# A linear-attention and MLP kernel on one core: the first kv in narrow columns, a quotient taken ahead, and loads moved

## Chip, core and metric

The kernel runs on one core of a Trainium2 chip. The metric is the device time of one execution in microseconds, the median of the runs shown. All arithmetic is float32.

## What is computed

The reference is an attention with a polynomial sketch as its feature map, followed by a layer norm and a two-layer MLP with a residual. Batch 4, 4 heads, sequence 1088, head size 32, r = 8, so 64 features; model size 128, hidden size 512.

```python
def phi(x):
    a = np.einsum('rd,bhsd->bhsr', S1, x)
    b = np.einsum('rd,bhsd->bhsr', S2, x)
    return np.einsum('bhsi,bhsj->bhsij', a, b).reshape(*x.shape[:-1], r * r)
q_p, k_p = (phi(q), phi(k))
kv = np.einsum('bhsf,bhsd->bhfd', k_p, v)
z = np.sum(k_p, axis=2)
num = np.einsum('bhsf,bhfd->bhsd', q_p, kv)
den = np.einsum('bhsf,bhf->bhs', q_p, z)[..., None] + 1e-06
x = (num / den)          # heads side by side: (B, S, 128)
...
xn = (x - mu) / np.sqrt(var + 1e-06) * g_ln
out = x + np.maximum(xn @ w_ch1, 0.0) @ w_ch2
```

## The kernel before

The program is written out by hand: every engine executes its instructions in the order in which the code emits them, and a wait of one instruction holds all that stand behind it on the same engine. The engines are TensorE (PE), VectorE (DVE), ScalarE (ACT), GpSimd (POOL) and SyncE (SP), which issues nearly all DMAs. DMAs of a queue share eight semaphores in turn, so that a DMA can also wait for the one eight places ahead of it.

The work is cut in two ways. Keys and values are taken by batch: for each of the four batches `key_rows` transposes the keys on DVE (tile kT), `key_features` multiplies them by the sketch on PE, `key_products` forms the 64 products per head and token (tile kp, mostly on POOL), `key_tokens` copies the values beside a column of ones (tile v), and `key_values` accumulates kv and z for the batch in one PSUM bank and copies the result to SBUF (kvz). The copy is made thrice: once as it stands, and twice with the two halves of the partitions exchanged[...].

Queries are taken in nine chunks of up to 512 tokens (two for each batch, and a last one with the 64 left over tokens of all four). For each chunk, query features are formed (from chunk 4 on by `token_products`, then through DRAM by `write_products` and `read_products`, tiles qo, qrows and qx). `numerators` multiplies them by kvz in 64x64 tiles on PE, and divides on DVE (tiles den, rden, x). `turn_x` or, through DRAM, `send_x` and `blocks_x` (tiles rows and xb) transpose x to xT; `hidden` is the first MLP layer (L620), `second` the second (L633), `result` adds the residual and sends the output.

At the start everything waits for loads. `load_rows`, `load_part`, `load_v` and `load_w1` issue them all at once on SyncE: batch 0's keys, queries and values, g, w1 in two halves, then w2, the rest of batch 0's queries, and batches 1 to 3 in order. w1 must be centred and scaled by g (`first_weight`). The weights come as 64-bit floats: the class `Rounded` splits each into a rounded float and a rest (methods `sizes`, `bound`, `terms`), and `one` adds the two. `busy` issues a multiplication without use, which fills TensorE's queue.

After that a loop runs over the slots c = 2 to 8. In slot c the kernel does the MLP of chunk c, the quotients of chunk c + 2, and the query products of chunk c + 4; keys enter beside it. The keys and values of batch 3 are transposed and copied at the end of slot 2 (`keys_in(3)`), their features and products are formed in slot 3 (`keys(3, ...)`), and their kv in slot 4 (`key_values(3, ...)`). In SyncE's order slot 2 is: outputs of chunk 1, qx of chunk 5, qrows of chunk 6, rows of chunk 4, xb of chunk 4, qx of chunk 6; then the outputs of chunk 2.

Of the kernel before, what the change touches and what calls it, by code (L numbers as in the profile page):

```python
# [10 lines left out]
U32 = mybir.dt.uint32  # L11
# [18 lines left out]
def kernel(  # L30
# [34 lines left out]
    nc = tc.nc  # L65
    P = 128
    B, H, S, D = q.shape
    R = S1.shape[0]
    DM = H * D
# [20 lines left out]
    def bank(i):  # L90
        return banks[:, 512 * i : 512 * (i + 1)]
# [14 lines left out]
    def load_rows(t, src, b, c0=0, c1=G * D):  # L106
        nc.sync.dma_start(  # L107
            out=t[b][:, c0:c1],
            in_=bass.AP(
                src.tensor, src.offset + b * H * S * D + c0, [[G * D, P], [1, c1 - c0]]  # L110
            ),
        )
# [41 lines left out]
    def load_w1(cols):  # L154
# [1 line left out]

    load_w1(slice(0, 256))
    load_w1(slice(256, DH))
    nc.sync.dma_start(
        out=w2_raw.rearrange("p (jc f) -> p jc f", f=DM),  # L160
        in_=moe_w_ch2.rearrange("(jc p) f -> p jc f", p=P),
    )
    load_rows(qn, q, 0, 512)
    load_rows(kn, k, 1)
    for b in range(1, B):
        if b > 1:
            load_rows(kn, k, b)
        load_v(b, nc.sync, lambda p0: 8 * p0, 8, 0)
        load_v_rest(b, nc.sync)
        load_rows(qn, q, b)  # L170


    class Rounded:
# [73 lines left out]
    def busy(n, at=0):  # L247
        nc.tensor.matmul(  # L248
            bank(at)[:, 0:n], ones, _ap(ones, 0, P, 0, [[0, n]]), start=True, stop=True
        )  # L250
# [55 lines left out]
    def key_tokens(b, part, eng, i0=0, i1=4):  # L306

        t0, n, m = (4 * part + i0, i1 - i0, P) if part < 2 else (8, 1, 64)
        o = _ap(v1s[b % 2], 0, m, t0 * W, [[W, n], [D1, H], [1, D]])
        i = _ap(vn[b], 0, m, D * t0 if part < 2 else 8 * DM,  # L310
                [[D, n], [8 * D if part < 2 else D, H], [1, D]])
        if eng is nc.scalar:
            eng.copy(o, i)
        else:
            eng.tensor_copy(out=o, in_=i)
# [31 lines left out]
    def key_values(b, at, t0=0, t1=NT):  # L347

        kvp, v1, kp, kvz = bank(at), v1s[b % 2], kps[b], kvzs[b]


        step = 64 if b == 0 else 32
        for t in range(t0, t1):
            m = P if t < 8 else 64
            for f in range(0, H * F, step):
                h, o = f // F, f % P
                nc.tensor.matmul(  # L357
                    kvp[o : o + step, D1 * (h // 2) : D1 * (h // 2 + 1)],
                    kp[0:m, H * F * t + f : H * F * t + f + step],
                    v1[0:m, W * t + D1 * h : W * t + D1 * (h + 1)],  # L360
                    start=(t == 0 and h < 2), stop=(t == NT - 1), skip_group_check=True,
                )
        if t1 < NT:
            return
        nc.scalar.copy(kvz[:, 0 : 2 * D1], kvp[:, 0 : 2 * D1])
        for i in range(2):
            nc.scalar.copy(  # L367
                kvz[F * i : F * i + F, 2 * D1 : W],
                kvp[F * (1 - i) : F * (2 - i), 0 : 2 * D1],
            )  # L370

    qTs, qos, qrs, qxs, qps = {}, {}, {}, {}, {}
    xs, rs, mvs, xTs, hTs, xbs = {}, {}, {}, {}, {}, {}
# [108 lines left out]
    def numerators(c):  # L482


        if c > LAST:
            return
        x = xs[c] = work.tile([P, 512], F32, tag="x", name="x", bufs=4)
        qp, n = qps.pop(c), ntiles(c) // 2
        step = 64 if c < LAST else 32
        for i in range(n):  # L490
            for h in range(H):
                for half in range(2):
                    rows = slice(F * half, F * half + F)
                    for u in range(0, P, step):
                        kvz = kvzs[CHUNKS[c][0] if c < LAST else u // 32]
                        t, o = 256 * h + P * i + u, W * i + D1 * h
                        z = D1 * (h // 2) + (0 if h % 2 == half else 2 * D1)
                        nc.tensor.matmul(  # L498
                            bank(half)[u : u + step, o : o + D1], qp[rows, t : t + step],
                            kvz[rows, z : z + D1], start=True, stop=True,  # L500
                        )
        den = small.tile([P, 4 * H], F32, tag="den", name="den")
        rden = small.tile([P, 4 * H], F32, tag="rden", name="rden")
        m = n * H
        nc.vector.tensor_scalar(
            out=_ap(den, 0, P, 0, [[m, 2], [1, m]]),
            in0=_ap(banks, 0, P, D, [[512, 2], [D1, m]]),
            scalar1=1e-6, scalar2=None, op0=ALU.add,
        )
        nc.vector.reciprocal(rden[:, 0 : 2 * m], den[:, 0 : 2 * m])  # L510
        for half in range(2):
            by_i, by_h = x_steps(c)
            nc.vector.tensor_tensor(  # L513
                out=_ap(x, 0, P, by_i * n * half, [[by_i, n], [by_h, H], [1, D]]),
                in0=_ap(banks, 0, P, 512 * half, [[W, n], [D1, H], [1, D]]),
                in1=_ap(rden, 0, P, m * half, [[H, n], [1, H], [0, D]]),
                op=ALU.mult,
            )
# [191 lines left out]
    key_tokens(0, 0, nc.gpsimd, 2, 4)  # L710
    key_tokens(0, 1, nc.vector)
    key_tokens(0, 2, nc.gpsimd)

    def rest():
        busy(128, 7)
        key_features(0, 2, 6)
        key_products(0, 2, nc.vector)

    query_features(0, rest)
    halves = [slice(0, 256), slice(256, 512)]  # L720
    w1_parts.sizes(halves[0], True)
    key_values(0, 7)
    busy(128, 4)

    g_terms = all_terms(g_raw, "g", 1)
    g_f = g_terms[0]
# [4 lines left out]
    nc.gpsimd.tensor_scalar(  # L731
        out=center, in0=ident, scalar1=-1.0 / DM, scalar2=g_f, op0=ALU.add, op1=ALU.mult
    )
    w1_parts.bound(halves[0], nc.vector)
    w1_term = one(w1_parts.terms(halves[0]), nc.vector)
    w1_parts.sizes(halves[1], True)
    w1_parts.bound(halves[1], nc.gpsimd)
    numerators(0)
    first_weight(halves[0], w1_term)
    turn_x(0)  # L740
    w2_parts = parts(w2_raw, "w2")
# [93 lines left out]
    for c in range(2, LAST + 1):  # L835

        b = (c + 3) // 2
        odd, some = c % 2 == 1, b < B
        if c == LAST - 1:
            blocks_x(LAST)  # L840
        if c < LAST:
            mlp_in(c, {
                1: lambda: key_values(b, 7, 0, 5), 3: lambda: key_values(b, 7, 5)
            } if some and not odd else {})
            root(c)
        if c == LAST - 1:
            root(LAST)
        numerators(c + 2)
        write_products(c + 4)
        send_x(c + 2)  # L850
        read_products(c + 4)
        if some and odd:
            keys(b, (2, 3, 7))
        statistics(c + 2)
        if c < LAST - 1:
            blocks_x(c + 1)
        if c == LAST - 1:
            second(c, 0, 3)
            result(c, 0, 3)
            mlp_in(LAST, {})  # L860
            second(c, 3, 4)
            result(c, 3, 4)
        else:
            second(c)
            query_rows(c + 5)
            result(c)
        token_products(c + 5)
        query_products(c + 3)
        if b + 1 < B and not odd:
            keys_in(b + 1)  # L870
# [30 lines left out]
```

## Time and profile before

| | us |
|---|---|
| median of 3 runs | 112.9 (112.32 to 114.01) |
| the profiled execution | 111.67 |
| its span, first to last instruction | 109.9 |
| TensorE busy | 102.4 (93%) |
| VectorE, GpSimd, ScalarE busy | 66.6, 49.1, 38.8 |

A profile is of one execution. "Busy" counts the time in which an engine has an instruction under way; fp32 products are done in two passes, so that TensorE has two records and two weight loads for each multiplication of the program. In a timeline a line gives the start from the beginning of the span, the duration, the engine, the line of the code, the operation, output and inputs, and how many instructions were merged; in brackets stands the idle time of the engine before it and what ended it. An engine with a q behind its name means its queue, such as SPq for DMAs issued. The chain is followed back from the last instruction, at each step to what released it; "issue" in it is time in which the engine waited for nothing that the profile shows. Line numbers are those of the code printed above.

### The profile page before, as it was taken

Reading aid. Unit: us, or ns where it says so; the run is one execution under the profiler, and the core shown is the slowest. Engines: PE = TensorE matmul, PEld = TensorE weight load, DVE = VectorE, ACT = ScalarE, POOL = GpSimd, SP = SyncE. Lnnn points to the kernel's source line nnn. Section 1 sums busy time; section 2 is a strip of 40 time slices with the busy share of each in tenths; the row PEclk is TensorE's granted clock in tenths of the full one; section 3 lists DMA queues with packets and bytes.
Section 4 is the critical chain, followed back from the end, with each engine's and each line's share of the span. In section 5 each row is a group of like instructions: output and inputs, shape, how many; then the busy total and the mean of one; then the engine's idle time right before and its main releaser. Section 6 shows DMA issues by size and latency. Waiting matters only on the chain.

```text
span 109.9 us, 4466 instructions
## 1 busy us (share of the span) xinstructions
PE 102.4 (93%) x1881; PEld 72.6 (66%) x1881; DVE 66.6 (61%) x196; ACT 38.8 (35%) x94; POOL 49.1 (45%) x139
## 2 busy tenths in 40 slices
PE   6899959999999799999999999999999999999960
PEld 3367825589745398855794698549829829839950
DVE  1776998994997476492389766707556546320330
ACT  5126317724557250225303530261062062062500
POOL 4065124006995099999443989702402404204000
PEclk9999999999999999999999999999999999999999
DMA  0999899999995206472987298518426434140032
GB/s 15 290 199 251 268 277 218 313 191 227 272 217 150 61 9 145 102 236 66 207 286 250 66 292 254 131 56 331 138 63 226 134 83 140 47 134 9 0 80 63
DMA packets 15155, 17.85 MB, mean 162 GB/s; under 512 B 3872, under 2 KB 10528, under 8 KB 15136
## 3 DMA queue, kind: packets, MB, share of 16 engines
q1 hardware_dynamic: 15040, 17.51, 58.8%
q8 instruction: 14, 0.23, 0.9%
q10 hardware_dynamic: 96, 0.07, 0.2%
q14 instruction: 5, 0.04, 0.2%
HBM read 11.54 MB, written 6.03 MB: 160 GB/s over the span
## 4 chain that ended last, share of the span: by engine, by line
PE 81%; DVE 5%; DMA 4%; SPq 3%; issue 2%; ACT 1%
PE banks L633 30%; PE banks L620 30%; PE banks L498 7%; PE banks L357 5%; DMA vn<-in_v_dram 4%; PE banks L322 3%; PE banks L403 3%; PE banks L429 2%; PE banks L580 1%; SPq L128 1%; DVE qp L412 1%; SPq L116 1%; DVE w_rest L687 1%; SPq L107 0%; ACT qb L411 0%
## 5 line engine op out<-in xcount | busy, mean ns | idle before, releaser
L623 ACT ACTIVATE hT<-banks 128x512 f32<-128x512 f32 (+1 forms) x36 | 20.7, 574 | 39.9 <-PE banks L620 39.8
L620 PE MATMUL banks<-xT,w 128*128 128x512 f32 (+1 forms) x74 | 34.0, 582 | 0.2 <-ACT xT L582 0.2
L633 PE MATMUL banks<-w,hT 128*128 128x128 f32 x272 | 33.7, 279 | 0.0
L633 PEld LDWEIGHTS banks<-w,hT 128*128 128x128 f32 x272 | 31.7, 192 | 2.0 <-issue 0.9
L620 PEld LDWEIGHTS banks<-xT,w 128*128 128x128 f32 x74 | 12.3, 189 | 11.0 <-ACT hT L623 5.3
L340 POOL TENSOR_TENSOR kp<-fs 128x1024 f32<-128x1024 f32 (+2 forms) x11 | 15.4, 1430 | 4.3 <-ACT fs L327 4.3
L648 DVE SCALAR_TENSOR_TENSOR ob<-banks,rstd,x 128x128 f32<-128x128 f32 x34 | 9.8, 343 | 10.3 <-POOL va L552 4.1
L498 PEld LDWEIGHTS banks<-kvz,qp 64*64 64x64 f32 (+1 forms) x576 | 9.0, 131 | 5.2 <-ACT kvz L367 2.5
L440 POOL TENSOR_TENSOR qo<-ft 128x512 f32<-128x512 f32 (+1 forms) x10 | 9.6, 980 | 5.7 <-DVE ft L434 5.7
L564 POOL TENSOR_TENSOR r<-va,r 128x4 f32<-128x4 f32 (+1 forms) x9 | 1.8, 200 | 20.9 <-DVE r L563 15.5
L563 DVE RECIPROCAL r<-r 128x4 f32<-128x4 f32 (+1 forms) x9 | 1.5, 176 | 15.5 <-ACT r L559 15.5
L357 PEld LDWEIGHTS banks<-v,kp 128*32 128x32 f32 (+3 forms) x504 | 7.0, 113 | 5.5 <-issue 4.6
L498 PE MATMUL banks<-kvz,qp 64*64 64x33 f32 (+1 forms) x576 | 10.1, 219 | 0.1
L357 PE MATMUL banks<-v,kp 128*32 128x33 f32 (+3 forms) x504 | 8.0, 202 | 0.7 <-issue 0.7
L538 DVE BATCH_NORM_STATS2 st<-x 128x6 f32<-128x128 f32 x34 | 7.3, 274 | 0.0
L248 PE MATMUL banks<-ones 128*128 128x256 f32 (+2 forms) x14 | 6.2, 555 | 1.0 <-DVE warm L144 1.0
L513 DVE TENSOR_TENSOR x<-banks,rden 128x256 f32<-128x256 f32 (+1 forms) x18 | 6.5, 403 | 0.3
L547 POOL TENSOR_TENSOR d<-st 128x4 f32<-128x4 f32 (+1 forms) x9 | 1.8, 201 | 10.5 <-DVE st L538 10.5
L477 DVE STREAM_TRANSPOSE qp<-qx 128x512 f32<-128x512 f32 (+1 forms) x10 | 5.9, 625 | 0.1
L322 PE MATMUL banks<-sk,kT 128*64 128x64 f32 x136 | 5.5, 227 | 0.4 <-DVE kT L291 0.4
L412 DVE TENSOR_TENSOR qp<-banks,qb 128x512 f32<-128x512 f32 x8 | 5.2, 683 | 0.9 <-ACT qb L411 0.8
L291 DVE STREAM_TRANSPOSE qT<-qn 128x512 f32<-128x512 f32 x8 | 5.5, 686 | 0.0
(77 smaller groups left out, 95.7 us busy)
## 6 DMA issues: line engine op xcount, KB each, us to landing
out_dram<-ob SPq DMA_DIRECT2D x33, 64.0 KB, 2.5
vn<-in_v_dram SPq DMA_DIRECT2D x16, 128.0 KB, 7.9
qrows<-qo SPq DMA_DIRECT2D x16, 128.0 KB, 3.2
qx<-qrows SPq DMA_DIRECT2D x4, 512.0 KB, 4.4
kn<-in_k_dram SPq DMA_DIRECT2D x3, 544.0 KB
qn<-in_q_dram SPq DMA_DIRECT2D x3, 544.0 KB
rows<-x SPq DMA_DIRECT2D x20, 64.0 KB, 2.0
xb<-rows SPq DMA_DIRECT2D x5, 256.0 KB, 3.1
```

The costliest lines, as they stand in the source:

```text
L322: nc.tensor.matmul(kf[u : u + 64, 64 * i : 64 * i + 64], kT[:, P * i + u : P * i + u + 64], sk, start=True, stop=True,)
L340: eng.tensor_tensor(out=_ap(kp, 0, m, (t0 + i0) * H * F, [[F, n], [R, R], [1, R]]), in0=_ap(kf, 0, m, o, [[R2, n], [1, R], [0, R]]), in1=_ ...
L357: nc.tensor.matmul(kvp[o : o + step, D1 * (h // 2) : D1 * (h // 2 + 1)], kp[0:m, H * F * t + f : H * F * t + f + step], v1[0:m, W * t + D1 ...
L412: nc.vector.tensor_tensor(out=_ap(p, 0, P, 256 * h, [[256, 2], [1, n]]), in0=_ap(banks, 0, P, 512 * h + 256, [[512, 2], [1, n]]), in1=own, ...
L440: nc.gpsimd.tensor_tensor(out=_ap(qo, 0, P, 32 * m * i, [[32, m], [R, 4], [1, R]]), in0=_ap(ft, 0, P, 4 * i, [[32, m], [1, 4], [0, R]]), i ...
L498: nc.tensor.matmul(bank(half)[u : u + step, o : o + D1], qp[rows, t : t + step], kvz[rows, z : z + D1], start=True, stop=True,)
L513: nc.vector.tensor_tensor(out=_ap(x, 0, P, by_i * n * half, [[by_i, n], [by_h, H], [1, D]]), in0=_ap(banks, 0, P, 512 * half, [[W, n], [D1 ...
L538: nc.vector.bn_stats(out=st[:, 6 * i : 6 * i + 6], in_=x_tile(c, i))
L620: nc.tensor.matmul(hp[:, cols], w1[:, P * j : P * (j + 1)], xTs[c][:, cols], start=True, stop=True)
L623: nc.scalar.activation(hTs[c][:, 512 * j : 512 * j + n], hp[:, 0:n], AF.Relu)
L633: nc.tensor.matmul(second_at(c, i), hT[:, 512 * j + P * i : 512 * j + P * i + P], w2[:, DM * j : DM * (j + 1)], start=(j == 0), stop=(j == ...
L648: nc.vector.scalar_tensor_tensor(out=ob[:, t], in0=second_at(c, i), scalar=rstd[:, i : i + 1], in1=x_tile(c, i), op0=ALU.mult, op1=ALU.add,)
```

## The change

- The first kv (batch 0) is done in 64 columns for the first four tiles of tokens only, and in 32 for the rest, as the other batches are.
- In the first quotient (chunk 0) the products that use the first copy of kvz stand ahead of those that use the exchanged copies. One exchanged copy for batch 0 is made on DVE, from kvz, instead of on ACT.
- The third part of batch 0's key products goes from DVE to POOL, and so does the sum of w1's two terms for the first half. The two fillers around the first kv are dropped; one of 512 columns is put behind the first quotient.
- A memset on POOL writes into w2's raw tile after the token copies of batch 0. So the load of w2 waits for it, and with it on SyncE's queue all later loads.
- Batch 3's keys and values are no longer loaded in the row of first loads, but in slot 2 of the loop, behind the read of qx. Batch 3's queries stay, directly behind batch 2's.

```diff
+    gate = w2_raw[0:1, 0:1].bitcast(U32)
+    def load_others():
+        nc.sync.dma_start(
+            out=w2_raw.rearrange("p (jc f) -> p jc f", f=DM),
+            in_=moe_w_ch2.rearrange("(jc p) f -> p jc f", p=P),
+        )
+        load_rows(qn, q, 0, 512)
+        for b in range(1, B):
+            if b < B - 1:
+                load_keys(b)
+            load_rows(qn, q, b)
+    def load_keys(b):
+        load_rows(kn, k, b)
         load_v(b, nc.sync, lambda p0: 8 * p0, 8, 0)
         load_v_rest(b, nc.sync)
-        load_rows(qn, q, b)
...
-        step = 64 if b == 0 else 32
         for t in range(t0, t1):
+            step = 64 if b == 0 and t < 4 else 32
...
         for i in range(2):
-            nc.scalar.copy(
-                kvz[F * i : F * i + F, 2 * D1 : W],
-                kvp[F * (1 - i) : F * (2 - i), 0 : 2 * D1],
-            )
+            o = kvz[F * i : F * i + F, 2 * D1 : W]
+            if i and b == 0:
+                nc.vector.tensor_copy(out=o, in_=kvz[0:F, 0 : 2 * D1])
+            else:
+                nc.scalar.copy(o, kvp[F * (1 - i) : F * (2 - i), 0 : 2 * D1])
...
+        order = [(i, h, half) for i in range(n) for h in range(H) for half in range(2)]
+        for i, h, half in sorted(order, key=lambda t: c == 0 and (t[1] + t[2]) % 2):
+            product(i, h, half)
...
     key_tokens(0, 2, nc.gpsimd)
+    nc.gpsimd.memset(gate, 0)
+    load_others()
     def rest():
-        busy(128, 7)
         key_features(0, 2, 6)
-        key_products(0, 2, nc.vector)
+        key_products(0, 2, nc.gpsimd)
     query_features(0, rest)
     halves = [slice(0, 256), slice(256, 512)]
     w1_parts.sizes(halves[0], True)
-    key_values(0, 7)
-    busy(128, 4)
+    w1_parts.bound(halves[0], nc.vector)
...
-    w1_parts.bound(halves[0], nc.vector)
-    w1_term = one(w1_parts.terms(halves[0]), nc.vector)
+    key_values(0, 7)
+    w1_term = w1_parts.terms(halves[0])
     w1_parts.sizes(halves[1], True)
     w1_parts.bound(halves[1], nc.gpsimd)
+    w1_term = one(w1_term, nc.gpsimd)
     numerators(0)
+    busy(512, 4)
     first_weight(halves[0], w1_term)
...
         read_products(c + 4)
+        if c == 2:
+            load_keys(B - 1)
         if some and odd:
             keys(b, (2, 3, 7))
```

`product(i, h, half)` holds the body of the three loops that stood in `numerators`, unchanged.

## Prediction before the run

> **What bounds the kernel now.** I read the page's chain first, then the chain in order of time, then the timelines of PE, DVE, POOL and SyncE around the places that the change touches.
>
> ```profile
> PE 81%; DVE 5%; DMA 4%; SPq 3%; issue 2%; ACT 1%
> DMA  0999899999995206472987298518426434140032
> ```
>
> From 16.89 us, when the first hidden layer starts, to 106.2 us the chain is TensorE work in program order with almost no gap. So a time is changed in two ways only: by when that work starts, or by a hole in it. The chain in order of time has two holes, neither ended by an engine:
>
> ```profile
> 15.27 0.90 issue
> 35.86 0.66 issue
> ```
>
> The TensorE records counted in order of time number 449 at the first hole and 1217 at the second: 768 apart, three times 256. The instruction DMAs of 16 KB (the page's queue q8, 14 packets) begin at 13.56 and 34.09 us, 2.60 and 2.43 us ahead of the ends of these holes. Both are TensorE waiting for its own instructions, fetched late because the DMA engines are full of loads (the 9s above, to 36 us).
>
> The second place is slot 3 of the loop (from 58 us), where batch 3's keys enter. TensorE from the chain, then DVE, POOL and SyncE from their timelines:
>
> ```profile
> 61.89 1.07 PE banks L498 x64
> 62.96 1.19 PE banks L322 x34
> 64.15 3.77 PE banks L633 x32
> ...
> 60.89 1.26 DVE L291 STREAM_TRANSPOSE kT<-kn 128x512 f32<-128x512 f32 x2
> ...
> 61.65 1.39 POOL L315 COPY v<-vn 128x512 f32<-128x512 f32 x3
> 64.12 4.44 POOL L340 TENSOR_TENSOR kp<-fs 128x1024 f32<-128x1024 f32 x3
> ...
> 54.47 0.75 DVE L513 TENSOR_TENSOR x<-banks,rden 128x256 f32<-128x256 f32 x2
> ...
> 58.28 2.60 SPq L593 DMA_DIRECT2D rows<-x  x4
> 62.25 0.34 SPq L601 DMA_DIRECT2D xb<-rows  x1
> 62.70 0.36 SPq L468 DMA_DIRECT2D qx<-qrows  x1
> 63.11 2.78 SPq L669 DMA_DIRECT2D out_dram<-ob  x4
> ```
>
> DVE transposes batch 3's keys at 60.89, TensorE uses them at 62.96. SyncE is late in this slot: it issues x of chunk 4 (ready at 55.2) at 58.28, and reaches the last read of slot 2 at 62.70.
>
> [...] w1's sum took 0.73 on POOL against 0.66 on DVE, kp of 64x256 0.62 against 0.41.
>
> **The change part by part.** Times are those of the profiled execution, 111.67 us with a span of 109.9, so 1.8 lie around it. The three runs' median is 112.9, 1.2 above.
>
> *Narrow columns.* The first kv is 72 passes of 64 columns in 2.36 us, 33 ns each. Later kv's are 144 passes of 32 in 0.83 + 0.82, 11.5 ns each. Now 32 x 33 ns + 80 x 11.5 ns = 1.97 us: 0.39 earlier, 80 more records, less 4 of a dropped filler.
>
> *First quotient.* ACT made three copies of kv one after the other (12.07 to 12.74). Products that need only the first now go first, and DVE makes the third copy (estimate 0.2, as ACT's of this shape). The 64 passes end near 13.0 instead of 13.91, if the instructions are there.
>
> *DVE and POOL.* DVE sheds the small kp (0.41) and w1's first sum (0.66), gains the copy (0.2) and a wait for ACT's first copy (about 0.35). So its w1 terms end at about 13.65 instead of 13.28, but the quotient follows at once instead of at 13.96: 0.3 earlier. The small kp on POOL (10.1 to 10.7) is done before TensorE needs it at 11.4. The sum on POOL ends at about 14.4; TensorE's w1 product waits for it and holds up the transposes of x behind it: about 15.1 against 14.94.
>
> *Fetch.* With 76 records more, number 449 falls inside these first 64 passes, reached near 12.4 instead of 14.99. [...] if the fetch starts at 11.3 and takes 2.5 us it holds TensorE from 12.4 to 13.8. The 512-column filler (0.87) behind then pushes the w1 product to 15.0. ACT's copies (0.37 and 0.37) follow, and the hidden layer starts at about 16.5: 0.4 earlier than 16.89. With a fetch as early as 10.4 it is 1.0; one that is as late as before (13.56) makes it 1.0 later. I take 0.4.
>
> *Gate.* A memset on POOL (0.1) after its last token copy (10.0) lets SyncE issue w2 at about 10.15 instead of 8.30. All 20 DMAs behind it are queued on SyncE. The w2 load landed at 14.28 and is read at 17.00; batch 1's keys landed at 17.98 and are read at 22.37. The engines still have w1's second half to move until 11 to 12, so the loads slip by under 1 us: nothing; 0.5 if the half of q0 read at 16.6 comes late.
>
> *Batch 3's loads, early side.* 1.1 MB less before 36 us; the hole of 0.66 at 35.9 mostly goes: 0.5 of gain, from 0 to 0.66.
>
> *Batch 3's loads, late side.* SyncE now issues kn and six DMAs of vn behind slot 2's qx read, at 63.1 on the old clock. All these times move with the gain, SyncE's too. That issue alone is 2.2 us after DVE's transposes and 0.1 after TensorE's use. It cannot go ahead of the read of xb, which waits for the landing of rows (62.18). How long the 544 KB take is bounded below by the 4.0 us of a 512 KB qx (67.1), above by adding 2.6 us to the landing of the out issued there (67.43): 70.0. With xb (256 KB) and qx (512 KB) just ahead, and the 338 GB/s of 64 to 66 us, qx ends at about 66.8 and 544 KB more take 1.6 to 2.5: I take 68.8. The first transpose takes 0.67: TensorE starts batch 3's features at 69.6, **6.6 us late**, with nothing else in its queue allowed ahead. Behind it stand second (3.77), the tokens (0.32), hidden 4. DVE's queue behind the transposes holds the reciprocal, quotient and statistics of chunk 5 and xT of chunk 4, ready at about 73, ahead of need. POOL's token copies wait for vn, 528 KB later at about 71.2; then come 1.39 + 1.1 + two kp parts of 1.96, to 77.6. At full clock TensorE wants the second part at 76.7, 0.9 too early. After 6.6 us idle I expect half clock for 3.4 us, which costs 1.7 and hides that 0.9; one of the two is paid. I take 1.7 and 0.15 for the transposes' pace: 8.45. Nothing later returns it, since TensorE is full to the end. Of the seven moved DMAs, vn delays slot 2's outputs by some 3 us; x of chunk 5 follows them, but its xT has over 9 us of slack.
>
> **Sum.** 111.67 - 0.4 - 0.5 + 8.45 = 119.2 on the profile's clock; on the runs' median 112.9 + 7.55 = 120.4.
>
> **Rivals** (medians)
> 1. *Long stall, as above*: 120.4. For it: the issue time, fixed by the order of SyncE's queue. Chance 0.58; own range 119 to 122.
> 2. *Shorter stall*: kn lands at the lower bound, 67.1, no half clock, 0.9 for kp: 4.9 + 0.9 less a gain of 1.2: 117.5. For it: little DMA between 60 and 63.5 us. Against: 768 KB directly ahead. Chance 0.27.
> 3. *Late fetch besides*: the fetch at record 449 starts as late as before (head 1.0 later), keys at 70.0, so stall 7.8 + 1.85: 112.9 + 1.0 - 0.5 + 9.65 = 123.0. Chance 0.09.
> 4. *Not slower*: SyncE runs so far ahead that the keys land by DVE's 60.9; then only the gains of 0.9 stay: 112.0. It decides if kn is issued by about 57. Against: kn stands behind xb, which waits for x of chunk 4, made at 54.5 to 55.2 and written in four issues of 0.45 and 2 us to land. At its very best that is 59.3. Chance 0.06.
>
> **Numbers.** The likeliest case gives 120.4 (the runs before spread from 112.32 to 114.01). The range 116.8 to 122.8 holds cases 1 and 2 and a part of 3. About 2% is what a measurement of this kernel tells from no change: slower by more 0.93, within 0.03, faster 0.04 (case 4 is split, since a larger head gain can join it).
>
> **What would show it.** Right: SyncE's kn of batch 3 issued behind the fourth qx; DVE's kT idle before it until DMA kn, 5 to 7.5 us; TensorE's L328 idle as long in the chain; POOL's token copies waiting for vn; second behind it with matmuls at up to twice the 112 ns spacing of now. At the start: a gap inside the first quotient's products, the first hidden layer near 16.5 us, no hole at 36. Wrong: L328 in slot 3 without a gap, or kn issued ahead of rows.

## The result, and the profile after

The changed kernel takes 120.61 us (median of 4 runs, 119.32 to 122.59) where the kernel before took 113.46 (4 runs, 112.32 to 115.26): slower, ratio 1.063, 95% interval 1.046 to 1.080. The forecast was 120.4. The profiled execution of the changed kernel is the one of 122.59 us, with a span of 120.8; it has a stretch of half clock near its start beside the large one. The four executions have mean granted clocks of 0.943 to 0.970; ratios with an interval compare the faster executions of both kernels, medians and ranges take all.

The page, first its span, then the granted clock in 40 slices of 3.02 us, then the chain's shares:

```profile
span 120.8 us, 4548 instructions
...
PEclk9999959999999999999999555799999999999999
...
PE 58%; DMA 15%; POOL 9%; SPq 7%; DVE 4%; issue 2%; ACT 1%
```

TensorE's share of the chain fell from 81% to 58%, DMA's rose from 4% to 15%. The clock, which was 9 everywhere, has a single 5 in the sixth slice and "5557" from the 23rd. The chain in order of time says what fills the second place (start, us, what):

```profile
62.82 0.34 SPq L475
...
63.20 7.36 DMA kn<-in_k_dram
...
70.59 0.72 DVE kT L297
...
71.36 2.18 PE banks L328 x34
73.54 5.30 PE banks L643 x32
```

SyncE reads qx (L475), issues kn directly behind it, and the path to the end leads through kn's landing 7.36 us later. The same stretch in the timelines of PE, DVE, POOL and SyncE:

```profile
62.81 1.14 PE L503 MATMUL banks<-kvz,qp 64*64 64x33 f32 x64
71.36 2.18 PE L328 MATMUL banks<-sk,kT 128*64 128x64 f32 x34 [7.42 <-DVE kT L297]
73.47 5.37 PE L643 MATMUL banks<-w,hT 128*128 128x128 f32 x32
...
80.15 0.90 PE L363 MATMUL banks<-v,kp 128*32 128x33 f32 x80
...
70.59 1.31 DVE L297 STREAM_TRANSPOSE kT<-kn 128x512 f32<-128x512 f32 x2 [8.89 <-DMA kn<-in_k_dram]
...
72.36 1.40 POOL L321 COPY v<-vn 128x512 f32<-128x512 f32 x3 [9.67 <-DMA vn<-in_v_dram]
...
74.72 4.43 POOL L346 TENSOR_TENSOR kp<-fs 128x1024 f32<-128x1024 f32 x3
...
63.20 1.26 SPq L107 DMA_DIRECT2D kn<-in_k_dram  x1
64.51 2.80 SPq L128 DMA_DIRECT2D vn<-in_v_dram  x6
```

L328, L503, L643 and L363 are the lines that were L322, L498, L633 and L357. TensorE is idle for 7.42 us before batch 3's key features; the features then take 2.18 us and second 5.37; in the same view of the kernel before they take 1.26 and 3.84. The query by windows (us, PE busy and count, PEld, DVE, ACT, POOL, granted clock, DMA share, GB/s) shows why:

```profile
64.00:66.00 2.00, 0.00 (x0) 0.00 (x0) 0.00 (x0) 0.00 (x0) 0.00 (x0) 1.00 0.82 259
66.00:68.00 2.00, 0.00 (x0) 0.00 (x0) 0.00 (x0) 0.00 (x0) 0.00 (x0) 0.62 0.85 244
...
74.00:76.00 2.00, 2.00 (x12) 2.00 (x11) 1.12 (x6) 0.00 (x0) 1.83 (x4) 0.50 0.77 223
76.00:78.00 2.00, 2.00 (x16) 2.00 (x16) 0.00 (x0) 0.00 (x0) 2.00 (x2) 0.82 0.20 52
```

The clock falls while TensorE waits, and is at half until 76.7 us, 5.3 us into the new work. The DMA engines are busy meanwhile, with shares of 0.82 and 0.85: xb and qx, 768 KB, were issued just ahead of kn. The trace has qx landed at 67.00, and kn 3.6 us after it.

The head of the changed kernel, PE's timeline:

```profile
11.74 0.67 PE L503 MATMUL banks<-kvz,qp 64*64 64x33 f32 x32 [0.34 <-ACT kvz L371]
14.00 0.67 PE L503 MATMUL banks<-kvz,qp 64*64 64x33 f32 x32 [1.59 <-DVE w_rest L224]
14.60 1.44 PE L254 MATMUL banks<-ones 128*128 128x512 f32 x2
15.84 1.06 PE L691 MATMUL banks<-w_rest,center 128*128 128x256 f32 x2
16.69 1.06 PE L590 MATMUL banks<-ident,x 128*128 128x128 f32 x4
17.78 0.80 PE L630 MATMUL banks<-xT,w 128*128 128x256 f32 x1
```

The first quotient is cut in two halves of 32 passes with 1.59 us between them. "DVE w_rest" stands as the releaser, but that instruction ends at 13.57 and the chain puts 0.43 us of "issue" behind it. The record behind the gap is number 449 (weight loads and semaphore records are counted too, and the count can be off by one), and the instruction fetch that brings it began at 10.88. Nor does the gap end with the exchanged copies of kvz, which the second half of the products needs: the last of them is done at 11.92, before the gap begins, and E5 and E10 below have the same order of products without a gap there. No trace shows when a line of instructions is asked for. "Asked for" in the expectations below is a name for a time that the traces have, the one at which TensorE reaches the record 256 places ahead of the line's first, here 9.8. From 15.3 us on the clock is at half for 3.4 us, and the first hidden layer starts at 17.78 instead of 16.89. The hole near 36 us is gone; 0.3 us is left at 39.95.

To compare kernels I cut each profiled execution at starts of a hidden layer (h0, h1, h3: first part of chunk 0, 1, 3; h4: second part of chunk 4). These cuts hold for all runs below.

| us | h0 | h0 to h1 | h1 to h3 | h3 to h4 | h4 to end |
|---|---|---|---|---|---|
| before | 16.89 | 13.11 | 28.04 | 12.02 | 39.83 |
| after | 17.78 | 13.54 | 27.70 | 21.96 | 39.83 |
| E1 loads back in front | 20.45 | 13.79 | 27.76 | 12.02 | 39.82 |
| E2 before, only the late load | 16.28 | 14.31 | 27.22 | 21.33 | 40.48 |
| E3 after, TensorE kept busy | 16.55 | 13.11 | 27.76 | 19.11 | 40.85 |
| E4 after, loads behind chunk 0's outputs | 16.05 | 13.11 | 30.61 | 12.02 | 39.83 |
| E5 E4 with columns of 64 | 16.82 | 13.10 | 28.65 | 12.02 | 39.82 |
| E6 E4 without the gate | 21.82 | 13.25 | 28.74 | 12.02 | 39.82 |
| E7 after, loads behind chunk 4's qx | 16.40 | 13.11 | 31.24 | 13.56 | 39.83 |
| E8 before, loads behind chunk 4's qx | 17.40 | 13.11 | 30.79 | 14.51 | 39.82 |
| E9 after, ScalarE issues the late loads | 17.67 | 13.68 | 27.48 | 16.47 | 43.69 |
| E10 E9 with columns of 64 | 16.12 | 13.11 | 27.22 | 16.14 | 39.83 |
| E11 before, ScalarE issues them late | 16.46 | 13.10 | 27.22 | 18.26 | 40.92 |
| E12 E11 with the gate | 16.05 | 13.20 | 27.23 | 16.47 | 41.74 |

The two profiled executions differ by 120.8 - 109.9 = 10.9 us of span: 0.89 in the head, 0.43 up to h1, -0.34 between h1 and h3, 9.94 in slot 3, nothing after it.

### The profile page after: what moved, and what is told of

Read it like the earlier page. It is cut to its first block, busy times and chain, and to the rows that moved or that the text cites. A ratio compares the mean times of both kernels' runs of the same rounds, so it can differ in the third digit from the quotient of the medians.

```text
span 120.8 us, 4548 instructions
## 1 busy us (share of the span) xinstructions
PE 106.3 (88%) x1919; PEld 75.6 (63%) x1919; DVE 65.6 (54%) x195; ACT 38.7 (32%) x93; POOL 50.8 (42%) x142
## 4 chain that ended last, share of the span: by engine, by line
PE 58%; DMA 15%; POOL 9%; SPq 7%; DVE 4%; issue 2%; ACT 1%
PE banks L643 22%; PE banks L630 19%; DMA kn<-in_k_dram 10%; DMA qx<-qrows 4%; PE banks L503 4%; POOL kp L346 4%; PE banks L363 4%; POOL qo L447 3%; PE banks L328 3%; PE banks L410 3%; SPq L462 2%; DMA rows<-x 2%; SPq L128 1%; SPq L679 1%; PE banks L254 1%
## 5 line engine op out<-in xcount | busy, mean ns | idle before, releaser
L643 PE MATMUL banks<-w,hT 128*128 128x128 f32 x272 | 35.2, 287 | 0.0
L643 PEld LDWEIGHTS banks<-w,hT 128*128 128x128 f32 x272 | 33.2, 199 | 2.0 <-issue 0.9
L633 ACT ACTIVATE hT<-banks 128x512 f32<-128x512 f32 (+1 forms) x36 | 20.7, 574 | 41.9 <-PE banks L630 41.9
L503 PEld LDWEIGHTS banks<-kvz,qp 64*64 64x64 f32 (+1 forms) x576 | 9.2, 131 | 7.2 <-issue 4.2
L328 PE MATMUL banks<-sk,kT 128*64 128x64 f32 x136 | 6.3, 249 | 7.5 <-DVE kT L297 7.4
L503 PE MATMUL banks<-kvz,qp 64*64 64x33 f32 (+1 forms) x576 | 10.3, 219 | 2.1 <-DVE w_rest L224 1.6
L328 PEld LDWEIGHTS banks<-sk,kT 128*64 128x64 f32 x136 | 5.5, 159 | 8.7 <-DVE kT L297 8.1
L297 DVE STREAM_TRANSPOSE kT<-kn 128x512 f32<-128x512 f32 x8 | 5.2, 686 | 8.9 <-DMA kn<-in_k_dram 8.9
L363 PEld LDWEIGHTS banks<-v,kp 128*32 128x32 f32 (+2 forms) x544 | 6.5, 111 | 4.8 <-issue 3.8
L254 PE MATMUL banks<-ones 128*128 128x512 f32 (+1 forms) x12 | 7.0, 710 | 1.0 <-DVE warm L144 1.0
L321 POOL COPY v<-vn 128x512 f32<-128x512 f32 (+2 forms) x8 | 3.5, 466 | 10.2 <-DMA vn<-in_v_dram 10.2
L333 ACT COPY fs<-banks 128x256 f32<-128x256 f32 (+1 forms) x12 | 3.5, 316 | 12.8 <-issue 10.5
L363 PE MATMUL banks<-v,kp 128*32 128x33 f32 (+2 forms) x544 | 7.4, 200 | 0.0
```

Source lines behind the costliest of these rows:

```text
L254: nc.tensor.matmul(bank(at)[:, 0:n], ones, _ap(ones, 0, P, 0, [[0, n]]), start=True, stop=True)
L328: nc.tensor.matmul(kf[u : u + 64, 64 * i : 64 * i + 64], kT[:, P * i + u : P * i + u + 64], sk, start=True, stop=True,)
L363: nc.tensor.matmul(kvp[o : o + step, D1 * (h // 2) : D1 * (h // 2 + 1)], kp[0:m, H * F * t + f : H * F * t + f + step], v1[0:m, W * t + D1 ...
L503: nc.tensor.matmul(bank(half)[u : u + step, o : o + D1], qp[rows, t : t + step], kvz[rows, z : z + D1], start=True, stop=True,)
L633: nc.scalar.activation(hTs[c][:, 512 * j : 512 * j + n], hp[:, 0:n], AF.Relu)
L643: nc.tensor.matmul(second_at(c, i), hT[:, 512 * j + P * i : 512 * j + P * i + P], w2[:, DM * j : DM * (j + 1)], start=(j == 0), stop=(j == ...
```

## The experiments

My theory: the late load is nearly all of the loss, through the place of kn in SyncE's queue; the rest of the change moves the head by the time at which an instruction fetch returns. The rivals: the head or the rearranged quotient carries part of the loss; the load would be late wherever it is issued in this slot, since the DMA engines are full.

**E1 and E2: the late load alone, and all but the late load.** E1 is the changed kernel with batch 3's loads in the first row; E2 is the kernel before with the late load.

```diff
E1 (against after)
-            if b < B - 1:
-                load_keys(b)
+            load_keys(b)
...
-        if c == 2:
-            load_keys(B - 1)
E2 (against before)
+        if c == 2:
+            load_rows(kn, k, B - 1)
+            load_values(B - 1)
```

> The changed kernel, with batch 3's keys and values issued in the first row of loads again, where they stood before; every other part of the change is kept. Theory (the late load makes the loss: a wait of TensorE in slot 3 and half clock after it): the wait of about 7 us and the cold stretch behind it go, and the time is that of before within 1.5 us: 112 to 114. What is left then is the start (hidden layer between 0.4 us earlier and 1 us later) and the hole near 36 us, which comes back. Rival (the start has grown, by the instruction fetch inside the first quotient and half clock after it, and makes a good part of the loss): still 2 to 4 us above before, 115 to 117.

> The kernel before, with one edit: batch 3's keys and values are loaded in slot 2, behind the read of qx, as in the changed kernel. Theory (late load): it shows the whole loss by itself, 7 to 9 us above before, with the wait of 6.5 to 7.5 us before batch 3's key features, and without the hole of 0.66 us near 36 us. Rival (the start makes a good part): 4 to 6 us above before.

Measured, against a kernel before of 112.48 us (7 runs, 110.2 to 116.27): E1 113.18 (110.92 to 115.64), no loss that can be told from none; E2 121.35 (121.15 to 121.88, so all four above the highest of the seven before), ratio 1.095, interval 1.082 to 1.108. In E2 kn is issued at 62.13 and lands at 69.61; TensorE waits as in the changed kernel:

```profile
70.40 2.18 PE L326 MATMUL banks<-sk,kT 128*64 128x64 f32 x34 [7.67 <-DVE kT L295]
72.51 4.49 PE L637 MATMUL banks<-w,hT 128*128 128x128 f32 x32
```

E1's slot 3 is 12.02 us, as before. So the late load alone makes the loss, and everything else together is about nothing in the median (0.7 us, well inside the spread of either kernel). E1's profiled execution has the worst head but one: the fetch of record 449 took 2.56 us, the quotient was held for 2.51, and the clock stayed at half for 6.8 us.

**E3: the half clock apart from the wait.** Eight multiplications of 512 columns without use stand ahead of batch 3's key features, so that TensorE is never idle.

```diff
         if some and odd:
+            for _ in range(8):
+                busy(512, 2)
             keys(b, (2, 3, 7))
```

> The changed kernel, with eight multiplications of 512 columns without use ahead of batch 3's key features in slot 3 (6.9 us at full clock), so that TensorE isn't idle while the keys come in. Theory (the wait is 6.6 to 7.4 us by the keys' landing, and the half clock after it costs 1.7 to 2.5 us more, of which up to 0.9 is given back as a wait for key products): the keys land when they did, and the time falls by 1 to 2 us against the changed kernel, to about 118.5 to 119.5. Rival (the half clock is hidden behind the key products, so that the idle time is all of the cost): no change, within 0.5 us.

Measured 120.19 us (119.02 to 122.03), ratio 1.074 with 1.045 to 1.103: in the time of whole runs this can't be told from the changed kernel. In the profile it can. PE's timeline (x16 for the eight, two records each):

```profile
62.27 7.16 PE L254 MATMUL banks<-ones 128*128 128x512 f32 x16
69.36 1.26 PE L328 MATMUL banks<-sk,kT 128*64 128x64 f32 x34
70.55 3.84 PE L643 MATMUL banks<-w,hT 128*128 128x128 f32 x32
```

No half clock: the features take 1.26 us instead of 2.18 and second 3.84 instead of 5.37. The half clock of the changed kernel is therefore worth 0.92 + 1.53 = 2.45 us. The stretch in slot 3 is 2.85 us shorter; the other 0.4 is a shorter wait, 8.16 us from the start of the quotient to that of the features instead of 8.55. kn landed 6.73 us after its issue, at 68.04, and its first transpose takes 0.7: the fillers, which end at about 69.4, may themselves hold the features up by 0.6. Later a hole of 0.74 that ends at 82.18, again at the start of a line of 256 records, gives back a part.

**E4: the same load earlier.** Batch 3's keys and values behind the outputs of chunk 0.

```diff
     result(0)
+    load_keys(B - 1)
...
-        if c == 2:
-            load_keys(B - 1)
```

> The changed kernel, with batch 3's keys and values issued right behind the outputs of chunk 0, ahead of the first write of query products: some 8 us later than before the change and 28 us sooner than in it. Theory: the transfer falls into the stretch from 34 to 40 us, where the DMA engines of the kernel before do little, lands before 41 us, 20 us ahead of its use, and leaves the instruction fetch of 30 to 36 us free: no wait in slot 3, no hole at 36 us; 0 to 1 us faster than with the loads in the first row, 111.5 to 113.5. Rival (a delayed load collides with the reads and writes of query products wherever it is put): a wait of over 1 us shows in slots 1 to 3, 114 or more.

Measured 113.05 us (112.06 to 114.3), ratio 1.017 with 0.996 to 1.037. kn is issued at 32.21 and lands at 36.44, slot 3 is 12.02 us again. But another stretch, h1 to h3, is 2.9 us longer than after's. PE's timeline:

```profile
36.71 0.90 PE L503 MATMUL banks<-kvz,qp 64*64 64x33 f32 x46
39.22 0.53 PE L503 MATMUL banks<-kvz,qp 64*64 64x33 f32 x18 [1.61 <-issue]
39.68 1.72 PE L328 MATMUL banks<-sk,kT 128*64 128x64 f32 x34
```

The gap ends at record 1473, a multiple of 256 behind 449. TensorE reaches the record 256 places ahead of it at 34.35, while the 1.1 MB are under way; the fetch starts at 36.51, 2.17 us later (0.81 in the changed kernel), and half clock for 3.4 us follows. The load left slot 3 and met the fetch.

**E5 and E6: narrow columns and the gate, on E4.**

```diff
E5 (against E4)
-            step = 64 if b == 0 and t < 4 else 32
+            step = 64 if b == 0 else 32
E6 (against E4)
-    nc.gpsimd.memset(gate, 0)
```

> The changed kernel with batch 3's loads behind the outputs of chunk 0 (as in the run before this one), and batch 0's first kv again wholly in columns of 64: 80 TensorE records fewer ahead of the first quotient. If the position of a multiple of 256 records decides (my theory): record 449 falls at the end of the first quotient or behind it, its line is there by 13.1 to 13.5 us and is wanted at 14 or later, so no hole in the head and no half clock, the first hidden layer at 15.6 to 16.4 us; and record 1473 is reached about 1.2 us later than with narrow columns, so the hole there of 1.61 us shrinks to 0 to 0.5 and the stretch from hidden 1 to hidden 3 takes 27.7 to 28.8 us instead of 30.61. If narrow columns are simply 0.39 us cheaper and the holes have another cause (rival): the hole in the first quotient stays at 0.4 to 0.5, the first hidden layer comes at 16.4 to 16.5, and the stretch stays at 30.6.

> The changed kernel with batch 3's loads behind the outputs of chunk 0, without the memset that gates w2 and all later loads. If the gate keeps the DMA engines free for the first instruction fetch (my theory): the fetch starts 2.5 to 3.5 us after its line is asked for instead of 0.77 (at 12.5 to 13.5 us), the first quotient is held for 1.9 to 3 us, half clock follows, and the first hidden layer comes at 18 to 20 us instead of 16.05. If the gate is without effect (rival, and what the prediction took): a hole of 0.4 to 1.6 us and the first hidden layer at 16.0 to 17.8.

Measured, against a kernel before of 112.21 (11 runs, 110.71 to 116.33): E5 112.58 us (111.22 to 114.21), E6 118.56 (115.35 to 120.53). E5: no hole in the quotient, no half clock; record 449 is now the first of the hidden layer, 5.8 us behind the start of its fetch. The hole at record 1473 is 0.78 us instead of 1.61, and that stretch 28.65 us. Both are as the position of the record wants it, though the hole shrank by less than I put. Its first hidden layer, at 16.82, is later than my 15.6 to 16.4; here the quotient itself starts 0.76 us later than in E4 (12.70 against 11.94), with the landings of the first loads. E6, PE's timeline:

```profile
12.64 0.67 PE L503 MATMUL banks<-kvz,qp 64*64 64x33 f32 x32 [0.34 <-ACT kvz L371]
17.00 1.08 PE L503 MATMUL banks<-kvz,qp 64*64 64x33 f32 x32 [3.68 <-issue]
18.01 2.07 PE L254 MATMUL banks<-ones 128*128 128x512 f32 x2
...
21.82 2.13 PE L630 MATMUL banks<-xT,w 128*128 128x256 f32 x6
```

Without the gate the quotient is held for 3.68 us and half clock lasts 6.8 us: the first hidden layer starts 5.8 us later than in E4, 0.7 of it because the quotient starts later, 5.1 behind that start. The memset that the prediction priced at nothing is what makes the rest of the head bearable. The trace shows how. The gate moves the issue of w2 only from 9.12 us (E6) to 9.96 (E4), but TensorE is 256 records ahead of record 449 at 10.7 and 10.0. In the nine kernels with the gate, w2 alone has been issued by that time, 0.02 to 0.21 us before it, and the fetch starts 0.39 to 1.11 us after it. In the five without it (before, E2, E6, E8, E11) the second half of q and batch 1's kn have been issued as well, in four of them also the first piece of vn, and the fetch starts 2.49 to 3.88 us after that time. The two ranges don't touch. Two pairs differ by the gate alone: E6 and E4, with 3.7 and 0.8 us, and E11 and E12, with 2.9 and 1.1.

**E7 and E8: the load in the middle.** Behind the first read of qx (chunk 4), in the changed kernel and in the kernel before.

```diff
     write_products(4)
     read_products(4)
+    load_keys(B - 1)
```

(In the kernel before the two calls that stand in `load_keys`; the loads elsewhere are dropped.)

> The changed kernel with batch 3's loads issued behind the first read of qx (chunk 4), about 44 us, when the fetch for record 1474 is over and 16 us before the keys are wanted. Theory: no wait in slot 3 (12.0 us from hidden 3 to hidden 4's second part), no hole of 1.6 us near 39, hidden 1 to hidden 3 in 27.4 to 28 us; with the first hidden layer at 16.0 to 17.8 a span of 108.7 to 110.5 and a median of 110.4 to 112.2, that is 0 to 2% below the kernel before. Rival: 1.1 MB at this place delay the fetch of the next line or the rows of chunk 3, and 0.5 to 1.5 us come back as a new hole between 46 and 55 us: median 112 to 113.5.

> The kernel before with this one edit: batch 3's keys and values loaded behind the first read of qx instead of in the first row. Theory: it keeps what the late load gave early (the hole at 36 us gone, first hidden layer at 16.3 to 16.9) without the wait in slot 3: hidden 1 to hidden 3 in 27.2 to 28 us, median 110.8 to 112.0 against 112.5 to 113.5 for the kernel before, a ratio of 0.98 to 0.995. Rival: the early gain belongs to chance in the fetches and a new hole takes its place: ratio 0.995 to 1.01.

Measured: E7 116.58 us (113.1 to 118.67), E8 116.76 (114.76 to 119.58), ratio 1.030 with 1.019 to 1.041. Both miss what I expected by 4 to 5 us. E7, SyncE's queue, PE and DVE:

```profile
43.46 1.15 SPq L107 DMA_DIRECT2D kn<-in_k_dram  x1
44.66 2.80 SPq L128 DMA_DIRECT2D vn<-in_v_dram  x6
47.55 5.08 SPq L603 DMA_DIRECT2D rows<-x  x4
52.74 3.17 SPq L462 DMA_DIRECT2D qrows<-qo  x4
56.08 0.34 SPq L611 DMA_DIRECT2D xb<-rows  x1
...
60.31 0.52 PE L436 MATMUL banks<-qT,wf 32*32 32x128 f32 x32 [2.59 <-DVE qT L297]
...
58.95 0.71 DVE L618 STREAM_TRANSPOSE xT<-xb 128x512 f32<-128x512 f32 x1 [2.91 <-DMA xb<-rows]
59.59 0.67 DVE L297 STREAM_TRANSPOSE qT<-qn 128x512 f32<-128x512 f32 x1
```

The keys are there in time. But the four writes of rows behind them take 5.08 us of SyncE (1.77 in the kernel before), because the second of them waits for the semaphore that kn's DMA holds (kn lands at 50.21, the second write goes out at 50.22), and xb of chunk 3 is issued at 56.08 instead of 52.65. DVE waits for it at xT; qT, which needs nothing of it, stands behind xT in DVE's queue, and TensorE waits for qT. It is the mechanism of slot 2 with other names: seven DMAs put into SyncE's queue push back what stands behind them. My rival named rows but priced it at 1.5 us at most. Its other half came true too: E7 has a hole of 0.89 us, ended by no engine, at record 2241 (52.16 to 53.04 us).

**E9 to E12: the same place in the program, another queue.** ScalarE has nothing to do from 54.55 to 60.24 us in the changed kernel; it issues the seven loads there.

```diff
E9 (against after)
-            load_keys(B - 1)
+            load_keys(B - 1, nc.scalar)
E10: E9 and   step = 64 if b == 0 else 32
E11: before, the seven loads in slot 2 by ScalarE
E12: E11 and the gate
```

> The changed kernel with batch 3's seven loads at the very same place of the program, but issued by ScalarE instead of SyncE. If the position in SyncE's queue, behind the reads of xb and qx, makes the keys late (my theory): ScalarE is done with its last instruction of that place at 54.55 us and idle until 60.24, so kn is issued at about 54.6 (in the changed kernel 63.20) and lands by 58.5 to 61, ahead of DVE's transposes; slot 3 takes 12.0 to 12.6 us from hidden 3 to hidden 4's second part instead of 21.96, no half clock there, and the median is 109.5 to 113. If these loads are slow at this place of the program whoever issues them, since they share the DMA engines with the traffic of rows, qx and qrows (rival): the keys land at 62 or later, or xb and qx come late in their place, and the stretch takes 14 us or more.

> As the run above (loads of batch 3 issued by ScalarE in slot 2), and batch 0's first kv wholly in columns of 64. If position of record 449 decides the head: no hole over 0.4 us in the first quotient, first hidden layer at 15.7 to 16.9 us, no half clock; hidden 1 to hidden 3 in 27.2 to 28 us, since nothing is loaded at 36 to 40; span 108.3 to 109.9, median 110 to 111.8, at or below the kernel before by 0 to 2%. Rival (narrow columns are a gain of 0.39 and nothing else): no better than the run above.

> The kernel before with this one edit: batch 3's keys and values issued by ScalarE in slot 2 instead of in the row of first loads. Theory: the early gain of the late load without its price: hidden 1 to hidden 3 in 27.2 to 27.5 us (28.04 before), slot 3 12.0 to 12.6 (21.33 with SyncE issuing them); the head as uncertain as before (first hidden layer 16.3 to 17.4, since the first fetch starts 2.5 to 3.9 us late): median 111 to 112.5, ratio 0.985 to 1.0. Rival: the loads in slot 2 delay xb or qx of the next chunks, and slot 3 takes over 13.5 us.

> The run above with the gate besides: a memset of w2's raw tile on GpSimd behind the token copies of batch 0, and w2 and all later loads behind it. Theory: the gate lets the first fetch start 0.6 to 1.2 us after its line is asked for, so the hole of 0.9 to 1.1 us ahead of the transposes of x goes, and the first hidden layer comes at 15.9 to 16.4 us: median 110 to 111.5, ratio 0.975 to 0.995. Rival: the loads that the gate holds back come late themselves (second half of the first queries, w2), and the first hidden layer stays at 16.9 or later.

Measured, against a kernel before of 112.86 (11 runs, 110.03 to 116.33): E9 118.53 us (117.58 to 120.96), E10 116.59 (114.19 to 119.33), E11 115.74 (113.62 to 117.73), E12 116.91 (115.55 to 118.66). All four miss. E9, the timelines of ScalarE, PE and DVE:

```profile
53.68 0.39 ACTq L107 DMA_DIRECT2D kn<-in_k_dram  x1
...
54.61 7.66 ACTq L128 DMA_DIRECT2D vn<-in_v_dram  x5
62.37 1.08 ACT L633 ACTIVATE hT<-banks 128x512 f32<-128x512 f32 x2 [8.01 <-DMA vn<-in_v_dram]
...
63.02 3.60 PE L630 MATMUL banks<-xT,w 128*128 128x512 f32 x4 [2.21 <-ACT hT L633]
...
62.81 1.30 DVE L484 STREAM_TRANSPOSE qp<-qx 128x512 f32<-128x512 f32 x2 [2.48 <-DMA qx<-qrows]
64.04 1.26 DVE L297 STREAM_TRANSPOSE kT<-kn 128x512 f32<-128x512 f32 x2
```

The half that concerns the keys is right: kn leaves at 53.68, 9.5 us earlier than in the changed kernel; its semaphore is free again at 60.14, when the third piece of vn goes out; DVE does not wait for kn (64.04 has no gap), and L328 starts without one. But the five last issues of vn take 7.66 us of ScalarE: the third piece waits on the semaphore that kn's DMA holds, as the second write of rows did in E7 (there eight DMAs behind kn, here three). Behind it stands the relu of the hidden layer (L633), which TensorE needs. And qx of chunk 5 takes 6.66 us to land, with 2.48 us of waiting on DVE. Slot 3's stretch is 16.47 us: less than half of the loss is left, moved from one queue to another. E10 to E12 lose in slot 3 as well (16.14 to 18.26 us), in two places: TensorE waits 1.16 to 1.86 us for the same relu, and 2.18 to 2.81 us ahead of chunk 8's query products, whose qT stands in DVE's queue behind an xT that waits over 4 us for its xb. The ends of E9, E11 and E12 are longer too: in E9 TensorE waits 2.06 us for chunk 5's xT, whose xb is late, and half clock follows from 87.14; in E11 half clock lasts until 77.25; in E12 TensorE waits 1.24 us for chunk 6's xT.

What these four settle is outside slot 3. Between h1 and h3, E10 to E12 take 27.22 or 27.23 us, like E2: 0.82 less than before, the whole early side of the late load when no fetch is late. In the head, E12 (before's code with the gate) takes 3.81 us from the end of the first kv to h0, E10 (the changed code with columns of 64) 4.43, neither held by a fetch. E10, PE's and POOL's timelines:

```profile
13.07 1.13 PE L254 MATMUL banks<-ones 128*128 128x512 f32 x2
14.69 0.70 PE L691 MATMUL banks<-w_rest,center 128*128 128x256 f32 x2 [0.48 <-POOL w_rest L697]
...
12.62 1.28 POOL L206 TENSOR_SCALAR w_cl<-w_cl 128x256 f32<-128x256 f32 x1 [1.52 <-ACT w_cl L195]
13.91 0.72 POOL L697 TENSOR_TENSOR w_rest<-w_up,w_rest 128x256 f32<-128x256 f32 x1
```

w1's sum on POOL stands behind POOL's bound for the second half (1.28 us), so TensorE's w1 product waits for it and holds up the transposes of x. The rearranged head is 0.6 us slower than the old one with the gate; its quotient ahead in line is paid back there.

No kernel here beats the kernel before by what its runs can show. The nearest is E5, at 112.58 against 112.21.

## Why the prediction was right, point by point

- **The issue of kn and what waits behind it**: right. Predicted at 63.1, behind the fourth read of qx; measured 63.20. The agreement to 0.1 us is luck in part: the prediction had this whole slot 0.9 us earlier than before, and chunk 3's hidden layer came 0.98 later. DVE idle, TensorE's features late, the token copies of POOL waiting for vn, all in the order given. Rival 4 (SyncE runs ahead) needed an issue by 57.
- **The landing of kn**: mis-sized. I took 68.8, that is 5.7 us from the issue; it was 7.36 here, 7.48 in E2, 6.73 in E3. The term came from the rate of 64 to 66 us of the kernel before: qx was to end at about 66.8 and kn some 2.0 us later. qx did land at 67.00; kn took 3.0 to 3.6 us more in these three, with vn issued beside it. The bound from above that I had named (70.0) was the better guide. So the wait was 7.42 us instead of 6.6. Rival 2's 67.1 was not met in any of the three.
- **Half clock**: right that it comes, too small. I took 1.7, from 3.4 us of work. It was 2.45, since the clock was at half for the first 5.3 us of work. In E2 it was at half for the first 3.5, and the same two groups lose 0.92 + 0.65 = 1.57, about what I had. The difference is where the work begins between two of the points at which the clock switched (see the last section): these lie whole pieces of 3.41 us apart, wherever work starts, and I had counted the 3.4 us from the start of the work. The trace of the kernel before shows half pace at the start, 0.85 us from one pass of 512 columns to the next at 2.06 us and 0.44 at 7.07, and no fall of the clock later: its longest hole in TensorE's work, 0.90 us, was followed by full clock. That the clock would fall after 6.6 us, and for how long, was an estimate that this trace did not show.
- **kp**: I took it as hidden by the half clock. POOL ends kp at 79.1 and TensorE wants it at 80.15: hidden, no cost. The 0.15 for the transposes' pace is 0.07 here.
- **The late side together**: 8.45 predicted; 9.94 in the profile, 7.42 + 2.45 + 0.07.
- **Early side**: 0.5 predicted; 0.34 in the profile, since a fetch at record 1473 leaves 0.3 us; 0.82 in E2 and E10 to E12. The first lies within my 0 to 0.66, the second above it.
- **Narrow columns**: 0.39 predicted; the first kv takes 2.08 us instead of 2.36, a gain of 0.28.
- **The fetch in the head**: the hole was predicted from 12.4 to 13.8 and came from 12.41 to 14.00. The step behind it failed. I let the filler take its 0.87 us and got the first hidden layer at 16.5. In the profiled execution the hole of 1.59 us was followed by half clock: the filler 1.44, the w1 product and the transposes 1.06 each, the first hidden layer at 17.78, 0.9 later than before instead of 0.4 earlier. In E3 and E4, where the hole is 0.41 and 0.46, it comes at 16.55 and 16.05. So the sign of the head depends on a microsecond of fetch, which my own range of -1.0 to +1.0 said and my single value did not.
- **The gate**: priced at nothing, right for the loads and wrong as an argument. It is worth 5.1 us in the head of E6, through the fetch. I had taken a fetch at 11.3 us (10.88 measured) without a reason; the gate is the reason.
- **DVE and POOL**: the sum on POOL was predicted to end at 14.4 and to hold up the product to 15.1; in E10 it ends at 14.63 and the product starts at 14.69. I saw the wait and did not set it against the gain of the quotient.
- **Counts**: 72 records more, not 76, since both fillers go; 18 DMAs behind w2, not 20; and rival 2 took off a gain of 1.2 where the sum has 0.9, so its 117.5 would be 117.8. Nothing hangs on these.

So the mechanism was right, and that the median came within 0.2 us is luck in part. For the profiled pair the same terms gave 7.55 us and 10.9 came, with nearly every term too small: by 1.5 in the late side, 1.3 in the head, 0.4 behind it and 0.2 in the early side. The profiled execution took 122.59 us where the median is 120.61. The medians can't settle the small parts: E2 alone loses 8.9 us, E1, which has the rest, 0.7, and the whole change 7.15, while the medians of the kernel before lie between 112.2 and 113.5 and its single executions between 110.0 and 116.3. How often the changed kernel's head meets half clock is open too, since only one of its executions has a profile. An estimate from spans and mean clocks (0.943 in the profiled one; 0.957, 0.970 and 0.969 in the others) gives 13.8 us at half clock in that one and 10.2, 7.1 and 7.3 in the others, so none of these had all that the profile shows.

## What to carry to other kernels

The load that was moved out of a busy stretch here was not free in any place that was tried later than chunk 0's outputs: it lost on SyncE's queue behind chunk 4's qx (116.58 us against 112.21) and in slot 2 (120.61 against 113.46), and in slot 2 on ScalarE's as well (118.53 against 112.86). Ask for the time at which such a load can be issued in its queue, what it pushes back there, and which semaphore it has to wait for. Where a program is long, count instructions and find out which piece of it stands where a new line of 256 records begins (here holes ended at 449, 1217, 1473 and 2241, whole multiples of 256 apart), and what loads have been issued when TensorE is 256 records ahead of it: two or three loads more by that time were worth 5.1 us in E6, more than the products that were reordered. And price an idle stretch of TensorE with the half clock behind it, which is not one number: 2.45 us in the changed kernel and 1.57 in E2.

## What the runs showed of the hardware

- Half clock came in pieces of one length: 3.4 us (the heads of the changed kernel and of E9, E4 near 40 us, E7 near 62, E9 at 63 and at 87), 6.8 (the heads of E1 and E6, slot 3 of E2 and E11, E8 at 60) and 10.2 (slot 3 of the changed kernel). In all fourteen traces every switch lies a whole number of 3.41 us pieces behind the trace's first switch to full clock (this comes at 4.13 to 7.01 us; in the changed kernel at 5.04, and 15.28 is three pieces on, 66.48 eighteen).
- What the clock did at such a point went with how busy TensorE was in the piece before. From full clock, all nine pieces inside the spans with TensorE busy for at most 1.36 us were followed by half clock, and none with 2.18 or more was; between 1.52 and 2.14 both occur, and what decides there is open. From half clock, the twelve pieces with 3.37 or more were followed by full clock, the seven with at most 2.83 by another piece at half. Some of them:

| piece, us | TensorE busy, of 3.41 us | clock in it | clock behind it |
|---|---|---|---|
| after, 63.06 to 66.48 | 0.88 | full | half |
| after, 66.48 to 69.89 | 0.00 | half | half |
| after, 69.89 to 73.30 | 1.94 | half | half |
| after, 73.30 to 76.72 | 3.42 | half | full |
| E2, 67.07 to 70.48 | 0.08 | half | half |
| E2, 70.48 to 73.90 | 3.42 | half | full |
| before, 14.37 to 17.78 | 2.11 | full | full |
| E4, 36.85 to 40.26 | 1.79 | full | half |

- So the length of one hole does not decide alone: half clock followed holes of 1.59, 1.61 and, in E9, 0.94 us, and not those of 0.90 (before), 1.09 (E8) or 2.55 (E10, at 70 us). And the changed kernel's features began 1.94 us ahead of such a point, and another piece at half followed (1.94 us busy in the table), where E2's began 0.08 us ahead of one and the next piece was busy throughout (3.42).
- The instruction fetch of record 449 started 0.4 to 1.1 us after TensorE reached the record 256 places ahead when w2 alone had just been issued (nine kernels), and 2.5 to 3.9 after it when q and kn, or these and vn, had been issued behind w2 (five). From the start of a fetch to the first instruction of the line passed 2.3 to 3.1 us in most holes, 4.05 in E1, where the fetch itself took 2.56.
- A DMA that had to wait for the semaphore of an earlier one held the issuing queue: 5.08 us for four writes on SyncE in E7 (1.77 before), 7.66 us for five loads on ScalarE in E9.
